# The first feed-forward product of the last 1024 tokens as seven half-size products, in the memory of attention

## The chip, the cores and the metric

The kernel runs on one core of one Trainium2 chip. The metric is the time of one execution on the device in microseconds (us); the kernel before takes 1391 us. A ratio is the mean time of one kernel's fast runs over that of the other kernel's fast runs in the same rounds, so it is not quite the ratio of the medians that stand beside it.

TensorE does the matmuls (PE in the profile, PEld its weight loads), VectorE is DVE, ScalarE is ACT, GpSimd is POOL. SBUF and PSUM are the on-chip memories in which the program has its tiles. The tiles that TensorE writes are in PSUM; they are counted in banks, as the program does: eight, each of 512 fp32 values (`BANK`) in every partition. The traces hold two records for each matmul (128 for the 64 matmuls of a block's plain first product), and "records" below are these.

## The reference

```python
# attention: q, k, v are (8, 8, 576, 64) fp32
scores = matmul(q, k.T) / sqrt(64)
scores = where(scores >= max(scores) - tau, scores, -1e9)
attn = softmax(scores)
x = matmul(attn, v)          # heads put side by side: 4608 tokens x 512
# feed-forward: w_in (512, 2048), w_out (2048, 512)
h = x @ w_in
g = h * (1 / (1 + exp(-1.702 * h)))
return g @ w_out
```

## The kernel before

Attention is done in 32 pairs of heads, the feed-forward in 18 blocks of 256 tokens that TensorE works on between the pairs' matmuls. A small scheduling model inside of the program, run when the program is built, puts the tasks into one fixed order for each engine.

The second product (`g @ w_out`) is already done by Strassen-Winograd's scheme: seven products of half size in place of eight, for which sums of quarters are formed before and after. Its seven products, in the order P1, P2, P6, P7, P4, P5, P3, go in turn to two banks:

```python
psA = tile_pool(name="psA", bufs=3, space=PSUM)   # [P, 2, 512]: a pair of banks each
psM = tile_pool(name="psM", bufs=2, space=PSUM)   # [P, 512]: one bank each
...
def mm1(blk, j, f):                               # first product, plain
    if f == 0:
        hidden[j] = psM.tile([P, BANK], FP32, name="hps", tag="mo")
    for c in range(NDC):
        nc.tensor.matmul(hidden[j][:, ts(f, BLK)], lhsT=w_in[:, c, ...],
                         rhs=xTs[blk][:, c, :], start=(c == 0), stop=(c == NDC - 1))
def gelu(j):                                      # one input in SBUF, one in PSUM
    nc.vector.scalar_tensor_tensor(out=g[:, :, j, :], in0=two(ths.pop(j)), scalar=1.0,
                                   in1=two(hidden.pop(j)), op0=ALU.add, op1=ALU.mult)
...
def product(x, js):                               # second product, one of seven
    left, right, k, o = PRODUCTS[x]               # k: which bank, o: which half of it
    if x == k and js[0] == 0:
        banks[k] = psM.tile([P, BANK], FP32, name="ops", tag="mo")
    for j in range(*js):
        nc.tensor.matmul(banks[k][:, ts(o, HM)], lhsT=left[:, j, :], rhs=right[:, j, :], ...)
```

## Time and profile before

| | before |
|---|---|
| time, median (range) | 1391.4 us (1391.3 to 1391.8) |
| span in the profile | 1391.0 us |
| last attention product ends at | 1176.7 us |
| last four blocks (14 to 17) | 1180.4 to 1387.6 us |
| of this, first product / second product of two blocks | 55.3 us / 48.3 us |

How the profile is read: busy shares say which engine is full, the slices say when, and the chain of waits says what each piece of the last-ending work waited for. The prediction shows these. Here is only the busy time in the stretch that the change concerns (the view of windows). After the stretch and its length come the busy us of TensorE, of its weight loads, of VectorE, ScalarE and GpSimd, each with its count of instructions, then the granted clock and the DMA's share and rate:

```profile
1180.20:1387.60 207.40, 207.37 (x961) 182.21 (x959) 33.49 (x60) 20.65 (x36) 44.29 (x56) 1.00 0.03 11
```

TensorE is busy for 207.37 of 207.40 us at a granted clock of 1.00, while VectorE has 33 us of work. It looks like a place where VectorE's time can be spent to save TensorE's.

### The profile page before, as it was taken

What the parts mean: (1) busy time and instruction counts of PE and PEld (TensorE: products, weight loads), DVE (VectorE), ACT (ScalarE), POOL (GpSimd) and SP (SyncE); (2) the same over time, 40 slices, a digit from 0 to 9 for tenths busy, and PEclk for the clock granted to TensorE, in tenths of its full rate; (3) what the DMA queues carried; (4) which work ended last, traced back from release to release, by engine and by line L of the source; (5) the groups of instructions that cost most, each with busy time, mean ns of one, the idle gap of its engine ahead of it and who ended that gap; (6) DMA issues with size and microseconds to landing.
All of it is one profiled execution on the core that took longest, in us unless ns stands there. A gap on an engine that the chain in (4) does not pass through costs nothing.

```text
span 1391.0 us, 18051 instructions
## 1 busy us (share of the span) xinstructions
PE 1341.9 (96%) x6856; PEld 1015.6 (73%) x6856; DVE 1053.8 (76%) x1776; ACT 634.4 (46%) x806; POOL 295.7 (21%) x374
## 2 busy tenths in 40 slices
PE   5778999999999999999999999999999999999999
PEld 3436864477777777777777777777777778888887
DVE  7989999978888888889888888888888887111111
ACT  5864663555454545454545445444545453100100
POOL 1121222212131213122212122131213121211211
PEclk9889999999999999999999999999999999999999
DMA  8774973201111111111111011111110100000000
GB/s 169 202 235 131 301 254 67 68 20 23 41 27 41 27 41 22 37 26 34 29 35 30 18 41 26 42 26 42 26 42 18 42 0 15 2 16 16 1 16 16
DMA packets 205377, 78.70 MB, mean 57 GB/s; under 512 B 192747, under 2 KB 192747, under 8 KB 205291
## 3 DMA queue, kind: packets, MB, share of 16 engines
q1 hardware_dynamic: 195723, 43.71, 14.9%
q0 software_dynamic: 7200, 33.55, 7.1%
q8 instruction: 54, 0.88, 0.3%
q10 hardware_dynamic: 2368, 0.30, 0.2%
q14 instruction: 32, 0.26, 0.1%
HBM read 68.05 MB, written 9.47 MB: 56 GB/s over the span
## 4 chain that ended last, share of the span: by engine, by line
PE 85%; DVE 9%; DMA 2%; SPq 1%; issue 1%; ACT 0%; POOL 0%; DVEq 0%; ACTq 0%; POOLq 0%
PE hps L601 32%; PE ops L691 28%; PE pv L519 9%; PE ps L383 8%; PE hps L641 4%; DVE part L420 2%; PE ps L376 2%; DVE s_m L490 1%; SPq L247 1%; PE den L519 1%; DMA arena<-in_moe_w_out_dram 1%; DVE arena L340 1%; DVE red L439 1%; DMA v_m<-in_v_dram 1%; DVE w_in L348 0%
## 5 line engine op out<-in xcount | busy, mean ns | idle before, releaser
L601 PE MATMUL hps<-xT,w_in 128*128 128x256 f32 x2048 | 457.5, 381 | 0.0
L601 PEld LDWEIGHTS hps<-xT,w_in 128*128 128x128 f32 x2048 | 385.1, 190 | 69.5 <-issue 18.5
L420 DVE TRANSPOSE_TENSOR_REDUCE part<-s_m 128x36 f32<-128x1152 f32 x228 | 304.6, 1354 | 71.2 <-ACT s_m L406 70.5
L406 ACT COPY s_m<-ps 128x576 f32<-128x576 f32 x240 | 141.2, 641 | 265.4 <-PE ps L383 264.1
L691 PE MATMUL ops<-w_out,arena 128*128 128x256 f32 x1024 | 234.1, 382 | 0.0
L610 ACT ACTIVATE th<-hps 128x512 f32<-128x512 f32 x144 | 85.5, 594 | 292.3 <-PE hps L601 271.5
L691 PEld LDWEIGHTS ops<-w_out,arena 128*128 128x128 f32 x1024 | 192.3, 190 | 36.1 <-issue 10.4
L669 POOL TENSOR_TENSOR arena<-arena 128x256 f32<-128x256 f32 x64 | 52.0, 812 | 610.8 <-DVE arena L613 610.8
L490 DVE TENSOR_TENSOR s_m<-s_m,mb 128x1152 f32<-128x1152 f32 x120 | 180.3, 1540 | 0.8
L691 PE MATMUL ops<-arena 128*128 128x256 f32 x768 | 171.0, 379 | 0.0
L383 PE MATMUL ps<-qkT 64*128 64x288 f32 x960 | 150.9, 436 | 19.6 <-DVE xT L586 9.3
L501 ACT ACTIVATE s_m<-s_m 128x1152 f32<-128x1152 f32 x120 | 137.3, 1156 | 66.4 <-DVE s_m L490 66.3
L613 DVE SCALAR_TENSOR_TENSOR arena<-th,hps 128x512 f32<-128x512 f32 x128 | 85.8, 671 | 100.9 <-ACT th L610 100.9
L691 PEld LDWEIGHTS ops<-arena 128*128 128x128 f32 x768 | 145.9, 190 | 19.8
L505 ACT ACTIVATE s_m<-s_m,shift,scl 128x1152 f32<-128x1152 f32 x120 | 158.4, 1339 | 1.4
L383 PEld LDWEIGHTS ps<-qkT 64*128 64x128 f32 x960 | 84.1, 189 | 78.0 <-issue 47.7
L519 PE MATMUL pv<-s_m,v_m 128*64 128x288 f32 x960 | 125.5, 413 | 2.2 <-issue 2.2
L713 DVE SCALAR_TENSOR_TENSOR osb<-ops,osb 128x256 f32<-128x256 f32 x112 | 44.4, 408 | 86.1 <-PE ops L691 85.7
L519 PEld LDWEIGHTS pv<-s_m,v_m 128*64 128x64 f32 x960 | 66.9, 138 | 55.9 <-issue 14.7
L676 POOL TENSOR_TENSOR arena<-arena 128x512 f32<-128x512 f32 x32 | 62.6, 1963 | 111.2 <-PE ops L691 111.2
L623 PE MATMUL ops<-w_out,arena 128*128 128x512 f32 x128 | 58.5, 608 | 1.6 <-DVE w_out L348 1.6
L671 POOL TENSOR_TENSOR arena<-arena 128x256 f32<-128x256 f32 x64 | 60.1, 938 | 0.0
(97 smaller groups left out, 1070.9 us busy)
## 6 DMA issues: line engine op xcount, KB each, us to landing
out_dram<-osb SPq DMA_DIRECT2D x36, 256.0 KB, 2.0
q_raw<-in_q_dram SPq DMA_DIRECT2D x120, 72.0 KB, 2.2
k_raw<-in_k_dram SPq DMA_DIRECT2D x116, 72.0 KB, 2.2
v_m<-in_v_dram SPq DMA_DIRECT2D x64, 128.0 KB, 2.4
w_out<-in_moe_w_in_dram POOLq DMA_DIRECT2D x12, 512.0 KB, 5.5
arena<-in_moe_w_out_dram POOLq DMA_DIRECT2D x12, 512.0 KB, 5.6
w_out<-in_moe_w_in_dram POOLq DMA_DIRECT2D x12, 511.6 KB, 6.8
arena<-in_moe_w_out_dram POOLq DMA_DIRECT2D x12, 511.6 KB, 6.7
```

The costliest lines, as they stand in the source:

```text
L383: nc.tensor.matmul(ps[:, h, 0:SH], lhsT=kT[ts(h, D), ts(t, P)], rhs=qT[ts(h, D), ts(c, SH)], start=True, stop=True,)
L406: nc.scalar.copy(out=o, in_=pss.pop((n, t, c))[:, :, 0:SH])
L420: nc.vector.tensor_reduce(out=o, in_=i, axis=AXL.X, op=op, apply_transpose=True)
L490: nc.vector.tensor_tensor(out=s, in0=s, in1=mb, op=ALU.subtract)
L501: nc.scalar.activation(out=s, in_=s, func=AF.Prelu, alpha=STEEP)
L505: nc.scalar.activation(out=s, in_=s, func=AF.Exp, scale=scl, bias=shift)
L519: nc.tensor.matmul(o[c][ts(h, D), 0:SH], lhsT=lhsT, rhs=rhs, start=(t == 0), stop=(t == NKT),)
L601: nc.tensor.matmul(hidden[j][:, ts(f, BLK)], lhsT=w_in[:, c, ds((f * HF + j) * P, P)], rhs=xTs[blk][:, c, :], start=(c == 0), stop=(c == N ...
L610: nc.scalar.activation(out=ths[j], in_=hidden[j], func=AF.Tanh, scale=GELU_SCALE / 2)
L613: nc.vector.scalar_tensor_tensor(out=g[:, :, j, :], in0=two(ths.pop(j)), scalar=1.0, in1=two(hidden.pop(j)), op0=ALU.add, op1=ALU.mult,)
L676: nc.gpsimd.tensor_tensor(out=u, in0=a12, in1=u, op=ALU.subtract)
L691: nc.tensor.matmul(banks[k][:, ts(o, HM)], lhsT=left[:, j, :], rhs=right[:, j, :], start=(j == 0), stop=(j == HF - 1),)
```

## The change

The intent: the first product of the last four blocks is done by the same scheme too, two blocks (512 tokens) at a time, which needs 7/8 of the matmuls. A product is cut into eight steps of 128 columns of each half of `w_in`; `j` counts them, and each j has its own P1 to P3. It needs room for sums of weights and inputs. This comes from attention's tiles, which are done by then: they move from a pool into one fixed buffer, `arena2`, and their memory is used again in the tail. (The profile leaves buffer numbers out and shows it as `arena`.) The core of the diff:

```diff
+    arena2 = const.tile([P, end], FP32, name="arena2")     # attention's tiles, then:
+    wc = [arena2[:, ts(x, WQ)]... for x in range(4)]       # sums of quarters of w_in
+    gs = [g, arena2[:, ds(gx_o, N_G)]...]                  # gelu of the second block
+    xsum = ...; hs = ...                                   # sums of x; h before the gelu
+    def w_sum(x, k, engine):                               # k = 0 VectorE, k = 1..3 GpSimd
+        o, a, b = (y[:, :, ts(k, 2 * P)] for y in W_SUMS[x][:3])
+        engine.tensor_tensor(out=o, in0=a, in1=b, op=W_SUMS[x][3])
...
+    def product1(blk, j, x):
+        if x == P1:
+            places[j] = psA.tile([P, 2, 512], FP32, name="ps", tag="ps")
+        k, o = PRODUCTS[x][2:]
+        for c in range(2):
+            nc.tensor.matmul(places[j][:, k, ts(o, BLK)], lhsT=left[:, c, ts(j, P)],
+                             rhs=right[:, c, :], start=(c == 0), stop=(c == 1))
+    def read1(j, x):           # P1: ScalarE copies; the others: VectorE adds ps to hs
...
+    def gelu1(j, h):           # both inputs in SBUF now
+        nc.vector.scalar_tensor_tensor(out=gs[h][:, :, j, :], in0=two(ths.pop((j, h))),
+            scalar=1.0, in1=hs[j % 2][:, :, h, :], op0=ALU.add, op1=ALU.mult)
...
-    def product(x, js):
+    def product(blk, x, js, w):
-        if x == k and js[0] == 0:
-            banks[k] = psM.tile([P, BANK], FP32, name="ops", tag="mo")
+        if x == P1 and js[0] == 0 and blk >= TAIL:
+            d = psA.tile([P, 2, 512], FP32, name="ps", tag="ps")
+            banks[blk] = [d[:, y, :] for y in range(2)]
+        elif x == k and js[0] == 0 and blk < TAIL:
+            banks[blk] = banks.get(blk, []) + [psM.tile([P, BANK], FP32, name="ops", tag="mo")]
```

More of the change, by code (lines that the diff above doesn't have):

```diff
@@ L126 @@
     NXT = 5
-    limits = {"psA": 3, "psM": 2, "s_m": 8, "s_t": 2, "io": 2, "osb": 2, "xT": NXT, "mb": 1,
+    limits = {"psA": 3, "psM": 2, "s_m": 8, "s_t": 2, "io": 2, "hs": 2, "osb": 2, "xT": NXT, "mb": 1,
               "raw0": 1, "raw1": 1, "qkT0": 1, "qkT1": 1, "v_m": 2, "w64": 2, "mbt": 1, "row": 1, "kd": 1, "rc": 1, "v_t0": 1, "v_t1": 1}
@@ L226, with seat, home, seat_scores @@
     offset.update({f"s_m{t}": (6 + 2 * t) * S for t in range(NKT)})
-    def home(n, tag, size, name, bufs, key=None):
+    room, end = {}, 0
+    for tag, size, bufs in (
+        ("s_m", 2 * S, 8), ("s_t", S, 2), ("raw0", S, 1), ("raw1", S, 1), ("qkT0", S, 1),
+        ("qkT1", S, 1), ("mb", 2 * S, 1), ("mbt", S, 1), ("rc", S, 1), ("v_m", NKT * 2 * D, 2),
+    ):
+        room[tag] = [(end + x * size, size) for x in range(bufs)]
+        end += bufs * size
+    arena2 = const.tile([P, end], FP32, name="arena2")
+    held = {}
+    def seat(tag, x=0):
+        o, size = room[tag][x]
+        return arena2[:, o : o + size]
+    def home(n, tag, key=None):
         if n in APART:
             o = offset[key or tag]
-            return spare[:, o : o + size]
-        return work.tile([P, size], FP32, name=name, tag=tag, bufs=bufs)
+            return spare[:, o : o + (2 if tag in ("mb", "s_m") else 1) * S]
+        return seat(tag)
+    def seat_scores(n, t):
+        if t < NKT and n in APART:
+            return home(n, "s_m", f"s_m{t}")
+        tag = "s_m" if t < NKT else "s_t"
+        o, size = room[tag].pop(0)
+        held[n, t] = tag, o, size
+        return arena2[:, o : o + size]
+    def free_scores(n, tiles=range(NKT + 1)):
+        for t in tiles:
+            if (n, t) in held:
+                tag, o, size = held.pop((n, t))
+                room[tag].append((o, size))
     def own(n, *pools):
@@ L241, in load_qk @@
         b, hp = divmod(n, NPAIR)
-        name, src = (("q", q), ("k", k))[which]
-        t = home(n, f"raw{which}", S, f"{name}_raw", 1)
+        src = (q, k)[which]
+        t = home(n, f"raw{which}")
         blocks = t.rearrange("p (c d) -> p c d", d=32)
@@ L254, in load_v @@
         b, hp = divmod(n, NPAIR)
-        t = work.tile([P, NKT, 2, D], FP32, name="v_m", tag="v_m", bufs=2)
+        t = seat("v_m", n % 2).rearrange("p (t h d) -> p t h d", t=NKT, h=2)
         for h in range(2):
@@ L356, in prep @@
     def prep(n, which):
-        dst = home(n, f"qkT{which}", S, "qkT", 1)
+        dst = home(n, f"qkT{which}")
         nc.vector.transpose(out=dst, in_=raws.pop((n, which)))
@@ L395, in keep @@
         if t == NKT:
-            st = work.tile([P, S], FP32, name="s_t", tag="s_t", bufs=2)
+            st = seat_scores(n, t)
             o = halves(st)
@@ L399, in keep @@
             if c == 0:
-                st = home(n, "s_m", 2 * S, "s_m", 8, f"s_m{t}")
+                st = seat_scores(n, t)
                 st = st.rearrange("p (h s) -> p h s", h=2)
@@ L432, in over_tiles @@
         stats[n, op] = r
+        if op == ALU.add:
+            free_scores(n)
     def over_groups(n, op):
@@ L462, in spread_max @@
     def spread_max(n):
-        mb = home(n, "mb", 2 * S, "mb", 1)
+        mb = home(n, "mb")
         nc.vector.transpose(
@@ L477, in row_in @@
     def row_in(n):
-        mb = home(n, "mb", 2 * S, "mb", 1)
-        mbt = work.tile([P, S], FP32, name="mbt", tag="mbt", bufs=1)
+        mb = home(n, "mb")
+        mbt = seat("mbt")
         row = rows.pop(n)
@@ L531, in values @@
         )
+        if n < NPAIR:
+            free_scores(n, tiles)
     def sums_by_pe(n, tiles, apart):
@@ L542, in sums_by_pe @@
         by_values(n, lambda t, h: ones, lambda h: ones_t[:, h, :], ps, tiles)
+        if not apart:
+            free_scores(n)
     def one_row(n):
@@ L567, in spread_sums @@
         nc.vector.reciprocal(out=r, in_=r)
-        rc = work.tile([P, S], FP32, name="rc", tag="rc", bufs=1)
+        rc = seat("rc")
         nc.vector.transpose(out=rc, in_=r.unsqueeze(2).to_broadcast([P, QB, 32]))
@@ L650, in gelu_0 @@
         )
-    qa = [[g[:, f, :, ts(h, HT)] for f in range(2)] for h in range(2)]
+    TAIL = NBLK - 4
+    WQ = NDC // 2 * HF * P
+    gx_o = 4 * WQ
+    xs_o = gx_o + N_G
+    hs_o = xs_o + 3 * NDC // 2 * BLK
+    assert hs_o + 8 * BLK <= end and BLK == 2 * P
+    wc = [arena2[:, ts(x, WQ)].rearrange("p (c f) -> p c f", f=HF * P) for x in range(4)]
+    gs = [g, arena2[:, ds(gx_o, N_G)].rearrange("p (f j t) -> p f j t", f=2, t=BLK)]
+    xsum = [
+        arena2[:, ds(xs_o + x * 2 * BLK, 2 * BLK)].rearrange("p (c t) -> p c t", c=2)
+        for x in range(3)
+    ]
@@ new lines @@
+    hs = [
+        arena2[:, ds(hs_o + x * 4 * BLK, 4 * BLK)].rearrange("p (f h t) -> p f h t", f=2, h=2)
+        for x in range(2)
+    ]
+    wq = [[w_in[:, ts(d, 2), ts(f, HF * P)] for d in range(2)] for f in range(2)]
+    W_SUMS = [
+        (wc[0], wq[1][0], wq[1][1], ALU.add), (wc[1], wc[0], wq[0][0], ALU.subtract),
+        (wc[2], wq[0][0], wq[1][0], ALU.subtract), (wc[3], wq[0][1], wc[1], ALU.subtract),
+    ]
+    def w_sum(x, k, engine):
+        o, a, b = (y[:, :, ts(k, 2 * P)] for y in W_SUMS[x][:3])
+        engine.tensor_tensor(out=o, in0=a, in1=b, op=W_SUMS[x][3])
@@ new lines, in x_quarter, with x_sum @@
+    def x_quarter(blk, d, h):
+        return xTs[blk + h][:, ts(d, 2), :]
+    def x_sum(blk, x):
+        b11, b12, b21, b22 = (x_quarter(blk, d, h) for d in range(2) for h in range(2))
+        u1, u2, u4 = xsum
+        o, a, b = ((u1, b12, b11), (u2, b22, u1), (b12, b22, b12), (u4, b21, u2))[x]
+        nc.vector.tensor_tensor(out=o, in0=a, in1=b, op=ALU.subtract)
+    places = {}
+    def product1(blk, j, x):
+        b11, b12, b21, b22 = (x_quarter(blk, d, h) for d in range(2) for h in range(2))
+        left, right = (
+            (wq[0][0], b11), (wq[0][1], b21), (wc[1], xsum[1]), (wc[2], b12),
+            (wq[1][1], xsum[2]), (wc[0], xsum[0]), (wc[3], b22),
+        )[x]
+        if x == P1:
+            places[j] = psA.tile([P, 2, 512], FP32, name="ps", tag="ps")
+        k, o = PRODUCTS[x][2:]
+        for c in range(2):
+            nc.tensor.matmul(
+                places[j][:, k, ts(o, BLK)], lhsT=left[:, c, ts(j, P)], rhs=right[:, c, :],
+                start=(c == 0), stop=(c == 1),
+            )
@@ new lines, in read1 @@
+    def read1(j, x):
+        (c11, c12), (c21, c22) = ([hs[j % 2][:, f, h, :] for h in range(2)] for f in range(2))
+        k, o = PRODUCTS[x][2:]
+        ps = places[j][:, k, ts(o, BLK)]
+        if x == P1:
+            nc.scalar.copy(out=c21, in_=ps)
+            return
+        sums = {
+            P6: [(c12, c21)], P2: [(c11, c21)], P7: [(c22, c12)], P4: [(c21, c22)],
+            P5: [(c12, c12), (c22, c22)], P3: [(c12, c12)],
+        }
+        for o, a in sums[x]:
+            nc.vector.tensor_tensor(out=o, in0=ps, in1=a, op=ALU.add)
@@ new lines, in tanh1 @@
+    def tanh1(j, h):
+        ths[j, h] = work.tile([P, BANK], FP32, name="th", tag="io", bufs=2)
+        nc.scalar.activation(
+            out=two(ths[j, h]), in_=hs[j % 2][:, :, h, :], func=AF.Tanh, scale=GELU_SCALE / 2
+        )
+    def gelu1(j, h):
+        nc.vector.scalar_tensor_tensor(
+            out=gs[h][:, :, j, :], in0=two(ths.pop((j, h))), scalar=1.0,
+            in1=hs[j % 2][:, :, h, :], op0=ALU.add, op1=ALU.mult,
+        )
+    qas = [[[y[:, f, :, ts(h, HT)] for f in range(2)] for h in range(2)] for y in gs]
@@ L653 @@
     qb = [[w_out[:, ts(f, HF), ts(m, HM)] for m in range(2)] for f in range(2)]
     s1, s2 = sg
-    s3, s4 = qa[1][0], s2
+    s4 = s2
     t1, t2, t4 = tw
@@ L666, in s_sums @@
     def s_sums(k):
+        qa = qas[0]
         a11, a21, a22, u1, u2 = (y[:, ts(k, 2), :] for y in (qa[0][0], qa[1][0], qa[1][1], s1, s2))
@@ L671, in s_sums, with s_sum1, s_last @@
         nc.gpsimd.tensor_tensor(out=a21, in0=a11, in1=a21, op=ALU.subtract)
-    def s_last(k):
-        a12, u = (y[:, ts(k, 4), :] for y in (qa[0][1], s2))
+    def s_sum1(x):
+        (a11, _), (a21, a22) = qas[1]
+        o, a, b = ((s1, a21, a22), (s2, s1, a11), (a21, a11, a21))[x]
+        nc.vector.tensor_tensor(out=o, in0=a, in1=b, op=ALU.subtract if x else ALU.add)
+    def s_last(k, w):
+        a12, u = (y[:, ts(k, 4), :] for y in (qas[w][0][1], s2))
         nc.gpsimd.tensor_tensor(out=u, in0=a12, in1=u, op=ALU.subtract)
@@ L680, with read @@
     PRODUCTS = [
-        (qa[0][0], qb[0][0], 0, 0), (qa[0][1], qb[1][0], 1, 0), (s2, t2, 0, 1), (s3, t3, 1, 1),
-        (qa[1][1], t4, 0, 0), (s1, t1, 1, 0), (s4, qb[1][1], 0, 1),
+        ((0, 0), qb[0][0], 0, 0), ((0, 1), qb[1][0], 1, 0), (s2, t2, 0, 1), ((1, 0), t3, 1, 1),
+        ((1, 1), t4, 0, 0), (s1, t1, 1, 0), (s4, qb[1][1], 0, 1),
     ]
     banks = {}
-    def product(x, js):
+    def product(blk, x, js, w):
         left, right, k, o = PRODUCTS[x]
-        if x == k and js[0] == 0:
-            banks[k] = psM.tile([P, BANK], FP32, name="ops", tag="mo")
+        if isinstance(left, tuple):
+            left = qas[w][left[0]][left[1]]
+        if x == P1 and js[0] == 0 and blk >= TAIL:
[3 more added lines that the diff above has]
+            banks[blk] = banks.get(blk, []) + [psM.tile([P, BANK], FP32, name="ops", tag="mo")]
         for j in range(*js):
             nc.tensor.matmul(
-                banks[k][:, ts(o, HM)], lhsT=left[:, j, :], rhs=right[:, j, :],
+                banks[blk][k][:, ts(o, HM)], lhsT=left[:, j, :], rhs=right[:, j, :],
                 start=(j == 0), stop=(j == HF - 1),
             )
-    def read(x):
+    def read(blk, x):
         if x == P1:
@@ L703, in read @@
         k, h = PRODUCTS[x][2:]
-        ps = banks[k][:, ts(h, HM)]
+        ps = banks[blk][k][:, ts(h, HM)]
         if x == P1:
@@ L842, in feed_forward, with second @@
                 sums.append(task("POOL", 2.5, FIRST, s_sums, j // 2, after=[gelus[j - 1], gelus[j]]))
+        second(blk, 0, {j: [gelus[j]] for j in range(HF)}, sums)
+    def second(blk, w, ready, sums):
         reads = [None] * 7
@@ L850, in feed_forward @@
             if x in (P1, P2, P4):
-                after += [gelus[j] for j in range(*js)]
+                after += [y for j in range(*js) for y in ready[j]]
             elif x == P3:
@@ L854, in feed_forward @@
             else:
-                after += sums[2 * p : 2 * p + 2]
+                after += sums[2 * (p % 2) : 2 * (p % 2) + 2] if w == 0 else sums[(P5, P6, P7).index(x)]
             after += [reads[y] for y in range(x) if PRODUCTS[y][2:] == PRODUCTS[x][2:]]
             ffn.append(task(
-                "PE", FFU / 4 * (js[1] - js[0]), LAST, product, x, js, after=after,
-                take=("psM",) if x in (P1, P2) and p == 0 else (),
+                "PE", FFU / 4 * (js[1] - js[0]), LAST, product, blk, x, js, w, after=after,
+                take=() if p else ("psA",) if x == P1 and blk >= TAIL
+                else ("psM",) if x in (P1, P2) and blk < TAIL else (),
             ))
@@ L865, in feed_forward @@
             if x == P6:
-                lasts = [task("POOL", 1.6, FIRST, s_last, k, after=ffn[-1:]) for k in range(2)]
+                lasts = [task("POOL", 1.6, FIRST, s_last, k, w, after=ffn[-1:]) for k in range(2)]
             if x == P1:
-                a = task("ACT", 0.35, FIRST, read, x, after=ffn[-1:], take=("osb", "osb"))
+                a = task("ACT", 0.35, FIRST, read, blk, x, after=ffn[-1:], take=("osb", "osb"))
             else:
                 a = task(
-                    "DVE", 0.84 if x == P5 else 0.42, FIRST, read, x, after=ffn[-1:] + reads,
-                    give=("psM",) if x >= P5 else (),
+                    "DVE", 0.84 if x == P5 else 0.42, FIRST, read, blk, x, after=ffn[-1:] + reads,
+                    give=(("psM",) if x >= P5 else ()) if blk < TAIL else ("psA",) if x == P3 else (),
                 )
@@ L876, in feed_forward, with two_blocks @@
             task("SP", 0.6, FIRST, store, blk, i, after=[reads[x]], give=("osb",), lag=2.2)
+    done_w, last_product1 = [], []
+    def two_blocks(blk):
+        b = -(-(blk + 1) * BLK // S) - 1
+        xs = [placed[n] for n in range(NP)]
+        first, xd = not done_w, []
+        for x in range(4):
+            if first:
+                done_w.append([task("DVE", 0.66, LAST - 1.0, w_sum, x, 0, nc.vector, after=done_w[-1:][0] if done_w else xs)])
+            after = (xd[-1:] or xs) + (done_w[x][:1] if first else []) + last_product1
+            xd.append(task("DVE", 0.66, LAST - 1.0, x_sum, blk, x, after=after))
+        if first:
+            for k in range(1, HF // 2):
+                for x in range(4):
+                    after = xs + done_w[x - 1][-1:] + done_w[x][-1:]
+                    done_w[x].append(
+                        task("POOL", 1.5, FIRST, w_sum, x, k, nc.gpsimd, after=after)
+                    )
+        last_product1.clear()
+        g1, sums = {}, []
+        for j in range(HF):
+            reads = [None] * 7
+            for x in range(7):
+                after = ffn[-1:] + [placed[n] for n in range(NPAIR * (b + 1))]
+                if x in (P6, P7, P5, P3):
+                    after += [done_w[{P6: 1, P7: 2, P5: 0, P3: 3}[x]][j // 2]]
+                if x in (P6, P7, P4, P5):
+                    after += [xd[{P6: 1, P7: 2, P4: 3, P5: 0}[x]]]
+                if x == P3:
+                    after += xs
+                after += [reads[y] for y in range(x) if PRODUCTS[y][2:] == PRODUCTS[x][2:]]
+                ffn.append(task(
+                    "PE", FFU / 2, LAST, product1, blk, j, x, after=after,
+                    take=("psA",) if x == P1 else (),
+                    give=("xT", "xT") if x == P3 and j == HF - 1 else (),
+                ))
+                if x == P1:
+                    a = task("ACT", 0.35, FIRST, read1, j, x, after=ffn[-1:], take=("hs",))
+                else:
+                    a = task(
+                        "DVE", 0.84 if x == P5 else 0.42, FIRST, read1, j, x,
+                        after=ffn[-1:] + reads, give=("psA",) if x == P3 else (),
+                    )
+                reads[x] = a
+            for h in range(2):
+                a = task("ACT", 0.6, FIRST, tanh1, j, h, after=[reads[P5 if h == 0 else P3]], take=("io",))
+                g1[j, h] = task(
+                    "DVE", 0.8, FIRST, gelu1, j, h, after=[a, last_mm2.get(j // 4), g1.get((j, 0))],
+                    give=("io", "hs") if h else ("io",),
+                )
+            if j % 2:
+                sums.append(task(
+                    "POOL", 2.5, FIRST, s_sums, j // 2, after=[g1[j - 1, 0], g1[j, 0]]
+                ))
+        last_product1.extend(ffn[-1:])
+        second(blk, 0, {j: [g1[j, 0]] for j in range(HF)}, sums)
+        again = [g1[j, 1] for j in range(HF)]
+        a = task("DVE", 1.3, FIRST, s_sum1, 0, after=again + ffn[-3:-2])
+        b = task("DVE", 1.3, FIRST, s_sum1, 1, after=[a] + ffn[-1:])
+        c = task("DVE", 1.3, FIRST, s_sum1, 2, after=[b])
+        second(blk + 1, 1, {j: [g1[j, 1]] for j in range(HF)}, [[a], [b], [c]])
@@ L993 @@
         while hp == NPAIR - 1 and (next_blk + 1) * BLK <= (b + 1) * S:
-            if next_blk >= PLAIN:
+            if next_blk >= TAIL:
+                if (next_blk - TAIL) % 2:
+                    two_blocks(next_blk - 1)
+            elif next_blk >= PLAIN:
                 feed_forward(next_blk)
```

## The prediction

"The lock" in it, and in the expectations below, is a name for this: some instructions of VectorE and sums of GpSimd last longer when they run side by side. The prediction's third view shows it: two instructions of L495 took 1.95 us beside a GpSimd sum of L669 that took 1.18, where the medians of one are 0.754 and 0.727 us.

> **What bounds the kernel now.** I read the busy shares first, then the slices, then the chain of waits in order of time, and then the instructions around the place where the change begins.
>
> ```profile
> PE 1341.9 (96%) x6856; PEld 1015.6 (73%) x6856; DVE 1053.8 (76%) x1776; ACT 634.4 (46%) x806; POOL 295.7 (21%) x374
> ...
> PE   5778999999999999999999999999999999999999
> PEld 3436864477777777777777777777777778888887
> DVE  7989999978888888889888888888888887111111
> ...
> PEclk9889999999999999999999999999999999999999
> ```
>
> TensorE is at 9 from the sixth slice to the end. In the last six slices VectorE is almost idle: 33.91 us busy of the 210.60 us after 1180.40. The granted clock there is 1.00. So the tail is TensorE's alone, and only fewer matmuls, with no wait added, shorten it. The chain of waits says what the tail consists of:
>
> ```profile
> 1171.71 5.00 PE pv L519 x40
> 1176.71 3.65 PE ops L691 x16
> 1180.37 27.63 PE hps L601 x128
> 1207.99 24.17 PE ops L691 x112
> 1232.17 27.63 PE hps L601 x128
> 1259.79 24.17 PE ops L691 x112
> ...
> 1363.39 24.19 PE ops L691 x112
> 1387.58 0.02 issue
> 1387.60 0.43 DVE osb L713
> ```
>
> The last pair's attention product ends at 1176.71. Then come 16 records of block 13, and then exactly the four blocks 14 to 17, each 27.63 us of first product (128 records, two to a matmul) and 24.17 us of second product (112 records, already seven half-size products). A record takes 27.63 / 128 = 0.2159 us. No wait stands between them. The four blocks which the change touches are just the four that nothing else runs beside: nothing that used to fill a wait of attention is taken away.
>
> [...] L613 has a median of 687 ns in the tail, L713 one of 424. [...] it makes me take the wait for a bank, not for half a bank, as the rule of the new loop. [...]
>
> ```profile
> 1128.00 1.95 DVE L495 TENSOR_TENSOR s_t<-s_t,mb 64x576 f32<-64x576 f32 x2
> 1128.15 1.18 POOL L669 TENSOR_TENSOR arena<-arena 128x256 f32<-128x256 f32 x1 [4.49 <-DVE arena L613]
> ...
> L490 DVE TENSOR_TENSOR s_m<-s_m,mb x120: 1314/1351/2441, 28.8 to 1161.7; 128x1152 f32<-128x1152 f32 x120
> ...
> L676 POOL TENSOR_TENSOR arena<-arena x32: 1263/2336/2398, 338.1 to 1373.9; 128x512 f32<-128x512 f32 x32
> ```
>
> L495 has a median of 0.754 us, so two should take about 1.4 and took 1.95; L669 has one of 0.727 and took 1.18. L490 goes from 1.35 to 2.44 at worst, L676 from 1.26 alone to 2.34.
>
> **What the change removes.** Two blocks of first product are 256 records. Seven products of two matmuls for each of 8 j are 7 x 2 x 8 x 2 = 224. That is 32 records fewer for each pair, 64 in all: 64 x 0.2159 = 13.8 us. This is the ceiling, and gives 1377.5 us.
>
> **What it adds.** For each j one ScalarE copy (0.38 us, as L706), seven VectorE additions from PSUM (7 x 0.42 = 2.94), two tanh (2 x 0.60) and two gelus (2 x 0.69): VectorE 4.3 us, ScalarE 1.6, against 28 records x 0.2159 = 6.04 of TensorE. By throughput it fits, so VectorE goes from 1 or 2 tenths to some 7. What counts is when each reading ends. One product now lasts only 4 x 0.2159 = 0.863 us, where it lasts 3.45 in the second product.
>
> ```profile
> 1373.38 3.43 PEld L691 LDWEIGHTS ops<-w_out,arena 128*128 128x128 f32 x16
> 1373.59 3.62 PE L691 MATMUL ops<-w_out,arena 128*128 128x256 f32 x16
> ...
> 1377.24 0.42 DVE L713 SCALAR_TENSOR_TENSOR osb<-ops,osb 128x256 f32<-128x256 f32 x1 [3.03 <-PE ops L691]
> ```
>
> A product's last record starts 0.65 us after its first and is modelled as ended 0.38 later; the reader starts 0.04 after that (1377.21 to 1377.24 here). So a reading starts 1.07 us after its product did and ends at 1.49. The next product in that bank comes 2 x 0.863 = 1.73 after, and its weights load 0.21 before. A prompt reader just makes it; a late one stops TensorE. From there, with time 0 at the first product of a j:
>
> 1. **Steady loop.** The last product of the j before is read at 0.20 to 0.62. Its second tanh follows at 0.72 to 1.32, about 0.1 for the handover. Only then can ScalarE copy the new first product: 1.27 to 1.65. The third product, in the same bank, should load weights at 1.52 and gets them at 1.70. I take 0.08 us of it as lost[...]. 7 j of 8 in two pairs: 14 x 0.08 = 1.1 us.
> 2. **Start.** The last place_x of attention ends at 1177.7, while block 13 keeps TensorE until 1180.4. In these 2.7 us VectorE does about four of its eight sums of weights and inputs (512 elements, some 0.62 start to start). The other four are mixed with the first readings; the fifth product needs the eighth sum, which I put 1.2 us late. Loss 1.2 us.
> 3. **The lock, weight sums.** Twelve GpSimd sums (128x512, 1.26 us as L676 alone) run from about 1184 to 1202, along the first three j. The gelus now read two SBUF inputs where L613 read one from PSUM. A gelu waits half a sum on average (0.63), and the second is blocked again by the next sum. I take a loss of 1 us for each of three j: 3 us.
> 4. **The lock, sums of gelu.** After an odd j GpSimd starts three sums of 0.73 us just when the second gelu wants to start. If GpSimd comes first, the gelu ends about 0.7 later, and the reading of the second product with it, and the fourth product stops for up to 0.58 us. Five such j are outside of point 3; half of them: 5 x 0.3 = 1.5 us.
>
> The weight sums are ready in time (each quarter is 4 x 1.26 = 5 us of GpSimd for 12 us of TensorE). The second pair's input sums and the three sums of the last block's second product lie beside 24 us of second product. All this costs nothing. The move of attention's tiles into one fixed buffer keeps sizes and counts, so I give it 0.
>
> Sum: 13.8 - 1.1 - 1.2 - 3.0 - 1.5 = 7.0 us gained, 1391.4 - 7.0 = 1384.4 us.
>
> **The rivals.** (a) Nothing blocks: if VectorE wins each race and the copy is in time, only the start's 1 us is lost: about 1378.5. For it speaks that the schedule was made with costs close to the measured ones; against it that the windows for a reading have no slack by the arithmetic above. (b) The readings become the bound of the whole loop: 0.1 us more at each of 112 products is 11 us, which leaves about 1389, and more would make it slower. For it speaks the same lack of slack; against it that only one reading in seven comes behind a tanh, and one behind a gelu. (c) Waits on halves of interleaved tiles that don't overlap: were the first tanh held until the fifth product's two readings are done, and the last reading until that tanh is done, each j would stop for 0.7 us, 10 us in all, 1388. Against it: GpSimd wrote its half of the gelu's tile at 1210.91 to 1211.64 while TensorE read the other half without a stop. (d) The fixed buffer changes waits in attention: TensorE is at 9 in nearly all slices, so what it could do is a few us either way, and nothing speaks for it.
>
> **Range and chances.** The ceiling is firm to within a few tenths, so the lower end is 1379.0, with a little for rival (a). The upper end, 1389.5, allows the stalls to be twice what I took. Faster by over 2% would be below 1363.5, past the ceiling: 0.005. Slower by over 2% needs stalls of 41 us: 0.01. Within 2%: 0.985.
>
> **What would show it.** In the profile of after, the chain should be unchanged to about 1180, and then show first products of 48.4 us plus stalls for each two blocks. Of 1.5 us or less in the second pair and 5 in the first, the theory would be right; equal stalls in both would say that GpSimd's weight sums are not the cause. The new gelus should have a median near 0.69 us and a worst of 1.3 or more in the first pair; if none is above 0.8, the lock (points 3 and 4) is wrong. TensorE's waits should name the ScalarE copy before the third product and VectorE's reading of the second product before the fourth. A first product at 48.4 us would mean that rival (a) holds; stalls spread over all products, rival (b). A chain that differs before 1176 would mean rival (d).

## The result, and the profile after

The changed kernel takes 1472.7 us (1471.4 to 1474.0, four runs) beside 1391.4 us of the kernel before; the ratio is 1.058 (95% interval 1.0565 to 1.0602). It is correct. It was expected to be 7 us faster and is 81 us slower.

First the page of after: busy shares of TensorE by slice, and the granted clock.

```profile
PE   5779999899999999999999999999999967887787
PEclk9899999999999999999999999999999979999999
```

TensorE's row was 9 to the end; now the last eight slices are at 6 to 8, and in one of them the clock is at 7. Then the view of windows, over the four parts of the tail: first product of blocks 14 and 15, their second products, and the same for blocks 16 and 17.

```profile
1178.85:1270.81 91.96, 64.36 (x226) 43.05 (x225) 41.71 (x83) 11.94 (x23) 14.36 (x14) 0.91 0.01 3
1270.81:1329.44 58.63, 51.47 (x226) 41.57 (x225) 15.02 (x25) 1.40 (x3) 8.37 (x7) 1.00 0.04 14
1329.44:1409.27 79.83, 59.05 (x226) 39.27 (x225) 32.20 (x68) 11.85 (x23) 7.38 (x9) 1.00 0.01 4
1409.27:1468.00 58.73, 51.47 (x224) 41.21 (x223) 11.68 (x22) 1.40 (x3) 7.54 (x7) 1.00 0.04 14
```

Each part has 224 records of matmul, as expected (the counts here are off by one or two at the edges), which take 224 x 0.2159 = 48.35 us without a wait. They took 91.96, 58.63, 79.83 and 58.73. The excess is 43.6 + 10.3 + 31.5 + 10.4 = 95.8 us. Take off the 13.8 us for the 64 records saved, and 1.4 us because the tail begins earlier (1178.85, not 1180.20), and what is left is the 80.3 us between the two spans (1391.0 and 1471.3), to 0.3. Two things stand out: the second products lose 10 us each two blocks although no matmul of theirs was changed, and the first pair of blocks loses 12.1 us more than the second.

How the loss looks from near is shown by the chain of waits over one j of the first product:

```profile
1202.62 1.15 PE ps L740 x4
1203.84 0.44 DVE arena L757
1204.32 1.15 PE ps L740 x4
1205.49 0.43 DVE arena L757
1205.97 1.15 PE ps L740 x4
...
1209.26 1.15 PE ps L740 x4
1210.43 1.10 DVE arena L757 x3
1211.61 0.63 ACT th L761
1212.24 0.30 ACT arena L750
```

TensorE and VectorE take turns: a product of four records, then a reading, then a product. One turn lasts 1.65 us (1204.32 to 1205.97) where a product alone takes 0.863. In this stretch no reading of VectorE runs beside a product of its own j, though successive products are in different banks. The readings are not slow: 0.42 us each, the size expected. What is off is when they start. The third product runs from 1202.62; the reading at 1203.84 is by the program's order that of the *second*, which had ended a whole product before.

The order of the program with its waits shows why. It is no profile, but a list of VectorE's instructions in one j of the changed kernel, with the product that each reads put in front:

```
P2      L757 TensorTensor arena2<-ps,arena2  [waits PE, Activation]
P6      L757 TensorTensor arena2<-ps,arena2  [waits PE]
P7, P4  L757 TensorTensor arena2<-ps,arena2  [waits DVE, PE] x2
P5      L757 TensorTensor arena2<-ps,arena2  [waits PE]
P5, P3  L757 TensorTensor arena2<-ps,arena2  [waits DVE] x2
```

The reading of P3, the last product, carries no wait on TensorE. It needs none, because the reading of P5 in front of it has already waited for P3. The waits that the trace itself records agree: the readings at 1205.49, 1207.13, 1208.78 and 1210.43 wait on the semaphore that TensorE raises at the end of each product, and the two after them (1210.77 and 1211.10) on VectorE's own alone. So a reading waits for the newest write into the whole tile, not for the one into its own bank, and the next write waits for the reading. This is the theory that the experiments test, as theory A.

The start of the tail has another reason. These lines are from the timeline of after:

```profile
1162.45 1.80 POOL L717 TENSOR_TENSOR arena<-w_in 128x512 f32<-128x512 f32 x1
...
1176.18 3.81 DVE L595 TENSOR_SCALAR r<-red 32x18 f32<-32x18 f32 x4
...
1181.21 0.95 DVE L623 TENSOR_TENSOR xT<-pv,arena 128x64 f32<-128x64 f32 x4
...
1187.20 2.04 PE L740 MATMUL ps<-arena 128*128 128x256 f32 x4 [6.46 <-DVE arena L726]
```

GpSimd's weight sums start at 1162, while the last pair is still in attention: they need nothing of it but free memory, and "after attention" stood only in the scheduling model. Beside them (1.3 us each here) VectorE's small row sums crawl: four instructions of 0.17 us (the median of L595) take 3.81, three of them some 1.2 each. The last placing, at 1176.76 in before, starts at 1181.21; TensorE idles for 6.46 us, and the four records after this take 2.04 us (1.03 in e8, below). The granted clock was 0.50 from 1187 to 1199 (by the trace's records of the clock, from 1184.4 to 1201.4).

### The profile page after: what moved, and what is told of

Its sections match the earlier page's. It is cut to its first block, busy times and chain, and to the rows that moved or that the text cites.

```text
span 1471.3 us, 18119 instructions
## 1 busy us (share of the span) xinstructions
PE 1360.3 (92%) x6792; PEld 998.2 (68%) x6792; DVE 1124.4 (76%) x1906; ACT 639.9 (43%) x822; POOL 299.5 (20%) x362
## 4 chain that ended last, share of the span: by engine, by line
PE 79%; DVE 15%; issue 2%; ACT 2%; SPq 1%; DMA 1%; DVEq 0%; ACTq 0%
PE hps L638 23%; PE ops L823 19%; PE pv L552 8%; PE ps L414 8%; PE ps L823 7%; PE ps L740 7%; PE hps L678 4%; DVE arena L757 3%; DVE part L451 2%; PE ps L407 2%; DVE arena L523 1%; SPq L278 1%; DVE osb L845 1%; PE den L552 1%; DVE red L472 1%
## 5 line engine op out<-in xcount | busy, mean ns | idle before, releaser
L451 DVE TRANSPOSE_TENSOR_REDUCE part<-arena 128x36 f32<-128x1152 f32 x236 | 315.2, 1354 | 71.3 <-ACT arena L437 70.5
L638 PE MATMUL hps<-xT,w_in 128*128 128x256 f32 x1536 | 346.3, 382 | 0.0
L638 PEld LDWEIGHTS hps<-xT,w_in 128*128 128x128 f32 x1536 | 287.9, 190 | 56.3 <-issue 18.5
L437 ACT COPY arena<-ps 128x576 f32<-128x576 f32 x288 | 171.1, 642 | 292.1 <-PE ps L414 271.1
L534 ACT ACTIVATE arena<-arena 128x1152 f32<-128x1152 f32 (+1 forms) x160 | 168.2, 1060 | 75.7 <-DVE arena L523 69.7
L538 ACT ACTIVATE arena<-arena,shift,scl 128x1152 f32<-128x1152 f32 (+1 forms) x160 | 194.3, 1243 | 1.9
L523 DVE TENSOR_TENSOR arena<-arena 128x1152 f32<-128x1152 f32 x128 | 190.6, 1527 | 0.9 <-DMA arena<-row 0.2
L414 PE MATMUL ps<-arena 64*128 64x288 f32 x1024 | 161.8, 439 | 21.9 <-DVE arena L390 11.1
L414 PEld LDWEIGHTS ps<-arena 64*128 64x128 f32 x1024 | 90.6, 191 | 84.7 <-issue 52.0
L552 PE MATMUL pv<-arena 128*64 128x288 f32 x960 | 126.0, 414 | 1.2 <-issue 1.2
L757 DVE TENSOR_TENSOR arena<-ps,arena 128x256 f32<-128x256 f32 x112 | 44.5, 421 | 95.4 <-PE ps L740 95.4
```

What stands on the lines that cost most here:

```text
L414: nc.tensor.matmul(ps[:, h, 0:SH], lhsT=kT[ts(h, D), ts(t, P)], rhs=qT[ts(h, D), ts(c, SH)], start=True, stop=True,)
L437: nc.scalar.copy(out=o, in_=pss.pop((n, t, c))[:, :, 0:SH])
L451: nc.vector.tensor_reduce(out=o, in_=i, axis=AXL.X, op=op, apply_transpose=True)
L523: nc.vector.tensor_tensor(out=s, in0=s, in1=mb, op=ALU.subtract)
L534: nc.scalar.activation(out=s, in_=s, func=AF.Prelu, alpha=STEEP)
L538: nc.scalar.activation(out=s, in_=s, func=AF.Exp, scale=scl, bias=shift)
```

## The experiments

Three theories were set against each other. **A**: a reading waits for the whole two-bank tile, so TensorE and VectorE take turns. **B**: 0.86 us is too short for a reading, whatever the tiles (the prediction's rival b). **C**: GpSimd's weight sums hold VectorE, and this is the main cost.

| run | what it is | us, median | ratio to before (95%) |
|---|---|---|---|
| after | the change | 1472.7 | 1.058 |
| e1_one_bank | both products in one-bank tiles | 1393.4 | 1.0006 (0.9996 to 1.0015) |
| e2_second_only | second product alone | 1452.3 | 1.0436 (1.0421 to 1.0452) |
| e9_first_only | first product alone | 1411.9 | 1.0145 (1.0127 to 1.0164) |
| e3_before_pair | before, with a two-bank tile | 1413.2 | 1.0158 (1.0141 to 1.0175) |
| e4_one_bank_gate | e1 and a gate for GpSimd | 1391.0 | 0.9992 (0.9983 to 1.0001) |
| e5_gate_only | after and the gate | 1472.2 | 1.0571 (1.0547 to 1.0595) |
| e6_memory_only | attention's tiles moved, nothing else | 1391.6 | 0.9997 (0.9988 to 1.0005) |
| e7_sums_first | e4, VectorE's sums first | 1383.4 | 0.9934 (0.9921 to 0.9948) |
| e8_th_psum | e7, tanh in PSUM | 1379.0 | 0.9903 (0.9889 to 0.9916) |
| e10_no_gate | e8 without the gate | 1390.2 | 0.9993 (0.9987 to 1.0000) |

All are correct. The kernel before had medians of 1391.3 to 1392.4 us in these rounds.

### e1: one tile for each bank

```diff
-        if x == P1:
-            places[j] = psA.tile([P, 2, 512], FP32, name="ps", tag="ps")
+        if x in (P1, P2):      # a tile for each bank; half of it stays unused
+            bank = psA.tile([P, 2, 512], FP32, name="ps", tag="ps")
+            places[j] = ([] if x == P1 else places[j]) + [bank[:, 0, :]]
...
-        if x == P1 and js[0] == 0 and blk >= TAIL:
-            d = psA.tile([P, 2, 512], FP32, name="ps", tag="ps")
-            banks[blk] = [d[:, y, :] for y in range(2)]
-        elif x == k and js[0] == 0 and blk < TAIL:
+        if x == k and js[0] == 0:   # psM in all blocks, as before
```

(The counts in the scheduling model that go with it are left out, here and below.)

> The changed kernel, but each of the two banks that a product alternates between is a tile of its own (first product: two tiles of the pairs' pool, half of each unused; second product: the two one-bank tiles of the kernel before). Same matmuls, same readings, same order of work. Theory A (a reading waits for the last write to its whole two-bank tile, and the next write for that reading, so that TensorE and VectorE take turns): the loss in steady state goes, that is 31.5 us in each of the two first products and 10.3 us in each two blocks of second product, 83.6 us; 1472.7 - 83.6 = 1389 us, with some 12 us of loss left at the start of the tail. Theory B (a product of 0.86 us is too short for any reading, whatever the tiles): the first product stays at about 10 us for each j, 1450 us or more. Theory C (GpSimd's weight sums hold VectorE): nearly no change, 1465 to 1475 us.

Measured: 1393.4 us, 79 us less than the change, some 4 us short of what was expected. Theories B and C are out as the main cause: the matmuls, readings and GpSimd's sums are the same, and in the two traces each of the four engines has its instructions in the same order. In its chain of waits the second products of blocks 14 and 15, 48.35 us by arithmetic, are one piece without a wait, and the first product of blocks 16 and 17 begins with two whole j, 56 records, without one:

```profile
1240.92 48.35 PE ops L821 x224
1289.27 12.15 PE ps L741 x56
```

### e2, e9 and e3: the two products apart, and the tile alone

e2 is the second hunk of e1 without the first, e9 the first without the second. e3 takes the kernel *before* and gives the second product of its last four blocks the two-bank tile:

```diff
 # e3, on the kernel before
-        if x == k and js[0] == 0:
+        if x == P1 and js[0] == 0 and blk >= NBLK - 4:
+            d = psA.tile([P, 2, 512], FP32, name="ps", tag="ps")
+            banks.update({y: d[:, y, :] for y in range(2)})
+        elif x == k and js[0] == 0 and blk < NBLK - 4:
             banks[k] = psM.tile([P, BANK], FP32, name="ops", tag="mo")
```

> The changed kernel, with only the second product of the last four blocks put back into the two one-bank tiles. Theory A: 4 x 5.15 = 20.6 us less, 1452 us. Theory B: this product lasts 3.45 us, long enough for a reading, so nothing changes: 1472 us. Theory C: nothing changes.

> The changed kernel with only the first product in one-bank tiles; the second product of the last four blocks stays in its two-bank tile. Theory A, with the two costs adding up: e1 plus what e3 added to the kernel before (21.4 us), 1393.4 + 21.4 = 1414.8 us; together with e2 this divides the loss: some 58 us for the first product, 21 for the second.

> The kernel before, with nothing changed but that the second product of its last four blocks goes into one two-bank tile of the pairs' pool in place of two one-bank tiles. Theory A: 4 x 5.15 = 20.6 us more, 1412 us. Theories B and C: no difference, 1391 us.

Measured: e2 1452.3, 20.4 us less than the change; e9 1411.9, 60.8 us less; together 81.2, and e1, with both, had 79.3. e3 made the kernel before 21.4 us slower. This is the cleanest run of all, since there is neither a new product nor a new sum in it, and 3.45 us of product hide any reading of 0.42 us that may start in time. Its chain of waits:

```profile
1213.19 3.73 PE ps L694 x16
1217.00 0.44 DVE osb L716
1217.58 3.71 PE ps L694 x16
```

TensorE's product ends, the reading comes, and only then the next product begins, as in the changed kernel. Taking turns costs here 21.4 / 4 = 5.4 us for a block.

### e5 and e4: the gate

GpSimd copies one element of VectorE's last weight sum before its own sums begin. It is a true wait, on data:

```diff
     def w_sum(x, k, engine):
+        if x == 0 and k == 1:
+            nc.gpsimd.tensor_copy(out=arena2[:, end - 1 : end], in_=wc[3][:, 0, 0:1])
```

> As e1_one_bank, and GpSimd first copies one element of VectorE's last weight sum, so that its twelve weight sums can't start before the last attention pair is placed and VectorE's own sums are done. Theory A with the lock as second cause: the last pair's row sums are no longer held, the last placing ends near 1176.5 in place of 1182, and the start of the tail loses some 4 us in place of 12: 1380 to 1385 us, 5 to 9 us less than e1. If the lock were of no account: the same as e1 within 1 us.

> The changed kernel with its two-bank tiles, and only the gate of e4 (GpSimd first copies one element of VectorE's last weight sum). Theory A: the turn-taking of TensorE and VectorE stays, and only the start is mended, as much as e4 gained on e1 (2 to 4 us): 1468 to 1471 us. Theory C as the main cause: 1400 us or less.

Measured: on the change (e5) the gate is worth nothing clear, 1472.2 us; its four runs lie far apart, at 1468.0, 1469.0, 1475.3 and 1476.0, and its profile is of the fastest. On e1 (e4) it is worth 2.3 us, less than expected, although the four small instructions are back at 0.71 us and the last placing at 1174.7. The timeline of e4 says where the rest went:

```profile
1172.50 0.71 DVE L595 TENSOR_SCALAR r<-red 32x18 f32<-32x18 f32 x4
...
1178.35 0.42 DVE L845 SCALAR_TENSOR_TENSOR osb<-ops,osb 128x256 f32<-128x256 f32 x1 [2.69 <-PE ops L823]
1178.69 0.68 DVE L719 TENSOR_TENSOR arena<-w_in 128x512 f32<-128x512 f32 x1
...
1182.87 1.10 PE L743 MATMUL ps<-arena 128*128 128x256 f32 x4 [2.83 <-DVE arena L728]
```

VectorE stood idle for 2.69 us in front of the reading of block 13's last product, with its first weight sum right behind. The scheduling model had put it so. Then TensorE waited for the sums, 2.83 us here and 2.15 a little later, and after the second wait its clock fell too (below, with e10).

### e7 and e8: towards a version that gains

e7 is e4 with three edits to the order: the reading of block 13's last product ranks behind the sums, the reading of P2 in the very first j comes after the last of them, and the scheduling model is told that a product waits for the reading of the one before it in its bank. e8 then writes the tanh to the two PSUM tiles that idle in the first product, so that the gelu has one input in SBUF, as in the kernel before:

```diff
-        ths[j, h] = work.tile([P, BANK], FP32, name="th", tag="io", bufs=2)
+        ths[j, h] = psM.tile([P, BANK], FP32, name="tps", tag="mo")
```

> As e4, with VectorE's order at the start mended: its eight first sums stand before the reading of block 13's last product and of the new second product, in the 2.7 us in which it idled in e4 (1175.7 to 1178.3), and the schedule knows that a product waits for the reading of the one before it in its bank. In e4 TensorE waited 2.8 and 2.2 us for two of these sums. If these waits are real costs of the order, 4 us less than e4: 1386 us, profile 1383. If another wait takes their place, no change.

> As e7, with the tanh written to the two one-bank tiles of PSUM that stand idle in the first product, so that a gelu reads one input from PSUM and one from SBUF, as in the kernel before. The lock as the cause of the rest: the gelus that took 1.19 us and more beside GpSimd go back to 0.69, the first pair's first product loses some 3 us less and the second's 0.6 less: 1382 us, profile 1379.5, faster than the kernel before by 0.7%. If the lock has no part in the rest: the same as e7.

Measured: e7 1383.4 us, better than expected; e8 1379.0 us, 4.4 us less again, where 4 had been expected. The gelus of e7 and of e8 (least, median and greatest duration in ns follow the count):

```profile
L769 DVE SCALAR_TENSOR_TENSOR arena<-th,arena x32: 679/691/1779, 1185.1 to 1330.4; 128x512 f32<-128x512 f32 x32
```

```profile
L769 DVE SCALAR_TENSOR_TENSOR arena<-tps,arena x32: 676/682/692, 1185.6 to 1327.0; 128x512 f32<-128x512 f32 x32
```

The worst falls from 1.78 us to 0.69, beside the same sums of GpSimd: for the gelus, what the prediction calls the lock is gone with the second SBUF input. The view of waits has a single wait of TensorE in e8 after 1170, of 0.6 us, and the first product of blocks 14 and 15 takes 48.73 us (1178.84 to 1227.57), their second products, with the wait, 49.37. The chain of waits, which the view follows back only to 1231.7, is TensorE alone from there:

```profile
1231.78 45.16 PE ops L823 x208
1276.94 48.35 PE ps L743 x224
1325.29 48.36 PE ops L823 x224
...
1373.67 0.42 DVE osb L845
```

e8 is faster than both kernels: ratio 0.9903 to the kernel before (1% only, but clear of the noise), 13.4 us by the medians of 1392.4 and 1379.0.

### e10 and e6: is the gate needed, and does the memory cost anything

> e8 without the gate on GpSimd's weight sums. If these sums, begun some 10 us before the last attention pair is placed, hold VectorE's row sums (as in the changed kernel, where single 0.17 us instructions took 1.2 us), the last placing comes some 4 us late, TensorE idles for about 5 us and its granted clock falls: 1386 to 1391 us. If the gate is of no use with the other two mends: 1379 us.

> The changed kernel with no block in the new first product (the four last blocks are done as before): attention's tiles in the one fixed buffer alone. My prediction gave this part 0: 1391.4 us. The pieces of the changed kernel's trace before 1176 run 1 to 2 us ahead of before's, so 1389 to 1391.5 us.

e10 is e8 without the copy; e6 is the change with `TAIL = NBLK`, so that no block takes the new way. Measured: e10 1390.2 us, so the gate is worth 11.2 us by the medians once the other losses are mended, or 12.4 when each run is set against the kernel before in its own rounds. Its timeline has the same lines as after's: the four small instructions at 1176.20 take 3.82 us, and TensorE idles for 6.49 us. The windows of e10 show the clock after this idling (the last figures but two of each line):

```profile
1180.00:1187.00 7.00, 0.77 (x4) 0.34 (x2) 6.83 (x11) 0.37 (x1) 5.88 (x4) 0.82 0.01 2
1187.00:1193.00 6.00, 5.13 (x11) 3.69 (x12) 3.94 (x9) 0.00 (x0) 0.00 (x0) 0.50 0.12 44
```

After TensorE's 6.49 us of idling the granted clock is 0.50 for six microseconds and more; in the stretch that holds most of the idling it is 0.82 on average. The length of one wait doesn't tell by itself what clock follows, as e5 and e4 show. After 2.81 us of idling e5 had 0.50 from 1183 to 1189 (first line below; by the trace's records from 1182.9, 2.1 us after the last matmul had ended). e4 after 2.83 us still had 0.97 in that stretch, but then 0.75 in the next, after its second wait of 2.15 us:

```profile
1183.00:1189.00 6.00, 4.12 (x8) 2.35 (x8) 3.41 (x7) 0.00 (x0) 1.98 (x3) 0.50 0.00 0
...
1183.00:1189.00 6.00, 3.85 (x15) 2.77 (x16) 4.42 (x7) 0.12 (x1) 3.67 (x4) 0.97 0.01 3
1189.00:1195.00 6.00, 5.71 (x20) 4.37 (x19) 4.25 (x7) 1.51 (x3) 5.92 (x5) 0.75 0.00 0
```

e6 gave 1391.6 us, the same as before: moving attention's tiles costs nothing, and the gain of up to 2 us that was thought possible did not come.

## Why the prediction was wrong, point by point

**What bounds the kernel and the ceiling: right.** The tail is TensorE's alone, 64 records less are worth 13.8 us (so the ceiling is at 1377.6, not 1377.5), and e8 gains 13.4.

**The step that failed** is the sentence "it makes me take the wait for a bank, not for half a bank, as the rule of the new loop". That rule was an assumption of mine, which no trace had shown. What the program waits for is neither of the two: its wait is for the tile, and the change put both banks into one (a turn of 1.65 us in place of 0.86, and 21.4 us in e3). So the arithmetic of 1.07, 1.49 and 1.73 us for a reading beside the next product was right for one-bank tiles (e8's second pair runs its 224 records in 48.35 us) and void for the kernel it was meant for. The loss by it: 31.5 us in each first product, 10.3 us in each two blocks of second product, which I had taken to be untouched. The diff shows the new tile in both places; the profile of before could not show its cost, as no two-bank tile there is written again after its first reading. That is a thing to look up in the code.

**Rival (b)** is nearest to what came. "The readings become the bound of the whole loop" is so, and "stalls spread over all products, rival (b)" is what the profile shows. The prediction's own sign said so too: the stalls of the two pairs, 43.6 and 31.5 us, are nearer to equal than to 5 and 1.5, so GpSimd's sums were not the main cause. Its size was off: 0.1 us for a product, where a turn loses 1.65 - 0.86 = 0.79, and the second pair 31.5 / 56 = 0.56 for each product on average. And its reason was another: no lack of time for a reading, as e1 shows, but a wait.

**Point 1, steady loop, 1.1 us: too much.** With one-bank tiles, and no gelu above 0.69 us, nothing is lost in e8's second pair (48.35 us). The readings last as the prediction had them: the median of L757, a tensor_tensor, is 424 ns, that of L713 in the kernel before, a scalar_tensor_tensor of the same size (128x256), 424 too.

**Point 2, start, 1.2 us: wrong in its order.** I had VectorE begin its sums at 1177.7 in idle time. In e4 it idled before them, and TensorE lost 2.83 + 2.15 = 5.0 us in two waits for them. Put in the order that I had assumed, in e7, no wait of TensorE for these sums is left, and e8's first product of blocks 14 and 15 loses 0.4 us in all.

**Points 3 and 4, the lock, 3.0 and 1.5 us: right in cause, wrong in place, and right in sum by luck.** e7 and e8 differ by it and by 4.4 us, where I had 4.5. Of this, e7's second pair loses 50.02 - 48.35 = 1.67 us in three odd j, 0.56 each: GpSimd comes first each time, where I took half. At this rate the five odd j of point 4 cost 2.8 us in place of 1.5. The 4.4 us are also net of 1.0 us that e8 loses anew in its first second products (49.37 us), so by estimate 4.4 + 1.0 - 2.8 = 2.6 us are left for point 3. What I overlooked is that the weight sums could begin before attention had ended, since only the scheduling model knew otherwise. There it was the row sums of the last pair that lasted longer (L595: 3.81 us for four, 0.71 with the gate in e4). L595 reads one SBUF tile, not two as the slowed gelus do; whether the cause is the same was not tested. In the changed kernel the first pair lost 12.1 us more than the second, the clock of 0.50 among it; e10 against e8 puts this start at 11.2 to 12.4 us.

**The memory, 0: right** (e6). **Rivals (c) and (d)** don't occur: e1's second pair has no stop of the kind of (c), and e6 excludes (d). **Rival (a)**, 1378.5 us (below the lower end of the range given, 1379.0), is in effect e8's 1379.0, but in a kernel whose tiles, order and lock had been mended first.

What stays open: why the gate by itself is worth nothing clear in e5 and 2.3 us in e4, when it is worth 11 to 12 in e8. In e5 as in e4 VectorE idles for 2.69 us before its first sum, and TensorE then waits 2.81 or 2.83 us for one of them. The trace's records of the clock show that the stretch at 0.50 lasts 17.1 us in the changed kernel, 10.2 in e1, e5 and e10 and 3.4 in e4, and that e7 and e8 have none. It is likely that the gain goes into these waits and the clock, but how much of it does was not measured.

## What to carry to other kernels

Where two engines are to work side by side on two banks of PSUM, look whether the banks are tiles of their own: in one tile the waits made the engines take turns (21.4 us in e3), and the trace showed it as readings that never ran beside a product. Work moved to an idle engine needs a true wait on data to stay where the schedule meant it to be (without it, e10 took 11.2 us more than e8), and what it does to the engines beside it counts as well as its own time: gelus of 0.69 us took up to 1.78 beside GpSimd's sums (e7). An engine that is nearly idle over a stretch isn't free at its start: look at what stands in front of the first instruction in its queue (in e4 VectorE's first weight sum stood behind a reading that it idled 2.69 us for).
